# An adaLN block with windowed attention and a spatial gMLP on one core: first loads over 128 partitions, wider PV and modulation streams, shared visits to 64-row tiles, and a newly searched issue order

## The chip, the cores and the metric

The kernel runs on one core of one Trainium2 chip. The metric is the time of one execution on the device in microseconds; below, the median of several executions. The profiled span is about 2 us shorter than the time of the same execution.

Most executions ran with TensorE's granted clock at 1.00 of full speed. Some had a lapse in it, and most of those were some 1 to 3 us longer. All traces that the argument rests on have a mean granted clock of 0.998 or more; the two that don't (e2, e7) are marked. The clock record leaves out the first microseconds: in the kernel before it begins at 7.38 us, and up to there that kernel started its 512-column matmuls 0.427 us apart, later 0.216. "Cold" and "warm" below are names for these two rates. Each batch of experiments ran on one chip, with executions of the kernel before in between; the three batches (e1 to e4, e5 to e8, e9 to e12) ran on three chips. The first batch had no changed kernel beside it, so its runs are compared by their ratio to the kernel before.

## The reference, cut to what matters

```python
# S = 2048 tokens, D = 448, 16 heads of 28, window 256
mod = silu(c) @ w_mod                     # six vectors of 448
sa, ca, ga, sb, cb, gb = mod
h = layernorm(x) * (1 + ca) + sa
x = x + ga * (windowed_causal_attention(h @ wqkv) @ wo)
h = layernorm(x) * (1 + cb) + sb
z = gelu(h @ w_in)                        # 1792 columns
z1, z2 = z[:, :896], layernorm(z[:, 896:])
g = w_sp @ z2 + b_sp                      # 2048 x 2048 over the tokens
return x + gb * ((z1 * g) @ w_out)
```

bfloat16 throughout.

## The kernel before

The program is a graph of some 1,500 named operations. A planner picks an engine and a place for each, by a table of priorities found by search (`PLAN`, 1,473 lines); every engine then runs its list in order. A new table therefore is a new issue order on every engine.

Feature chunks are four of 112 rows. Weights are loaded over 112 partitions:

```python
def wload(name, prio, dst, w, a, b, o=None, ks=(0, KC), eng="sp"):
    src = w[ks[0] * KP:ks[1] * KP, a:b].rearrange("(c p) n -> p c n", p=KP)   # KP = 112, KC = 4
    ...
x_load(0, 2, -90)
t_wmA = mload("wmodA", -89.9, 0, 2)                                   # modulation, columns 0 and 1
t_wqk = [wload("wqk0", ...), wload("wqk1", ...)]
x_load(2, 4, -89.6); t_wv = wload("wv", -89.35, ...); x_load(4, 8, -89.4)   # in the order of these priorities: x tiles 4 to 7 before wv
```

TensorE runs 15 warm-up matmuls in one piece, the first modulation (32 matmuls of one column), then 5 more. The weighted sums of attention (PV) stream 29 columns, 28 of V and one of ones.

After attention comes what I call the **z stage**: the two halves of `h @ w_in`. The features 0 to 383 are three full-height matmuls per output tile. The last 64 rows (the *rest*) of two output tiles run side by side in the two 64-row halves of the array: the two matmuls of a pair start 3 to 4 ns apart, and with 448 columns a pair takes 0.19 to 0.20 us, where one full-height stream takes 0.189. A stay in the 64-row mode is a *visit*:

```python
def unit(name, pr, outs, n):          # outs: four output tiles; z2m = second half, z1m = first half
    for i, (ten, sub, lhs, rhs, ...) in enumerate(outs):      # parts name_0 .. name_3
        for kc in range(3): mm(..., lhs(0, 128, kc), rhs(0, 128, kc), kc == 0, False)
    # then name_r, the rest, ends all four accumulations
    for i, ... in enumerate(outs):
        p0 = 64 * (i % 2)
        mm(..., lhs(p0, p0 + 64, 3), rhs(p0, p0 + 64, 3), False, True, tile_position=(p0, 0))
```

The **mixer** follows: 448 matmuls of 512 columns (`w_sp @ z2`), and the 112 of the output product.

The softmax here doesn't subtract the row's maximum and nothing guards it: scores larger than these inputs give would overflow.

Of the kernel before, what the change touches and what calls it, by code (L numbers as in the profile page):

```python
# [5 lines left out]
BF16 = mybir.dt.bfloat16  # L6
# [238 lines left out]
c -173.9192 -1  # L245
x0 -178.4461 -1
wmodA -9.5493 -1
wqk0 -85.9193 -1
wqk1 -146.8247 -1
x2 -221.2408 -1  # L250
wv -106.8604 -1
x4 -53.1809 -1
wmodG -38.8077 -1
wo -96.1295 -1
x8 -204.0347 -1
x12 -87.9443 -1
wmodB0_0 -132.3998 1
wmodB0_1 -108.5096 25
wmodB0_2 -147.1130 13
wmodB0_3 -114.1850 25  # L260
wmodB1_0 -138.0143 22
wmodB1_1 -43.9367 8
win0_0 -76.8442 26
win0_64 -80.4809 33
win1_0 -191.2469 4
win1_64 -169.0191 13
win2_0 -98.4862 7
win2_64 -58.2163 0
win3_0 -78.8290 14
win3_64 -9.8098 40  # L270
wout0 -55.9687 44
wout1 -0.2256 35
wout2 -220.9180 31
wout3 -169.1615 41
wz -132.5927 -1
id1 85.2723 -1
id2 26.3866 -1
nh -98.3075 -1
xpad -185.4513 -1
wqk0m -43.1282 -1  # L280
va1 -109.7318 -1
opad -127.2002 -1
dsilu -214.1979 -1
silu -77.6433 -1
dexp -98.0973 -1
scr1 -60.2104 -1
warm0 35.9475 -1
modA -36.2363 -1
warm1 -16.3154 -1
modAe0 4.7110 -1  # L290
modAe1 -30.8303 -1
gateA 30.4838 -1
wog0 -52.7600 -1
wog1 129.5466 -1
wog2 20.8828 -1
wog3 -105.6927 2
wqkc0 -106.7042 -1
wqkc1 -99.4673 -1
wqkc2 64.2122 -1
wqkc3 -24.9916 -1  # L300
l1_0st0 -65.9727 -1
l1_0ag -12.7322 -1
l1_0ve -55.7842 -1
l1_0rs -22.6614 -1
xn0 18.1777 -1
l1_1st0 34.6470 -1
l1_1ag -80.7040 -1
l1_1ve 1.4062 -1
l1_1rs -59.9654 -1
xn1 -73.4046 -1  # L310
tr0_0_0 -75.9896 -1
tr0_0_1 -88.3166 -1
hT0_0 41.5631 -1
tr0_1_0 -171.6096 -1
tr0_1_1 43.3804 -1
hT0_1 42.2614 -1
tr0_2_0 -146.6143 -1
tr0_2_1 -8.7731 -1
hT0_2 73.1086 -1
tr0_3_0 36.1564 -1  # L320
tr0_3_1 -15.9541 -1
hT0_3 -16.1573 -1
qk0_0_0 -23.3584 -1
qk0_0_1 -19.3486 -1
qk0_0_2 -26.0578 -1
qk0_0_3 -169.2100 -1
qke0_0 -62.0930 -1
qk0_4_0 -171.1839 -1
qk0_4_1 -124.5527 -1
qk0_4_2 -143.9112 -1  # L330
qk0_4_3 -61.6511 -1
qke0_4 -108.6858 -1
qk0_1_0 -15.9474 -1
qk0_1_1 30.7340 -1
qk0_1_2 -9.1455 -1
qk0_1_3 29.9306 -1
qke0_1 -85.4446 -1
qk0_5_0 74.2985 -1
qk0_5_1 59.0211 -1
qk0_5_2 8.9765 -1  # L340
qk0_5_3 -11.9115 -1
qke0_5 -122.3120 -1
qk0_2_0 11.7421 -1
qk0_2_1 -41.2138 -1
qk0_2_2 -128.5694 -1
qk0_2_3 -161.7595 -1
qke0_2 -104.6116 -1
qk0_6_0 -30.1175 -1
qk0_6_1 -86.6129 -1
qk0_6_2 10.7182 -1  # L350
qk0_6_3 -76.7948 -1
qke0_6 -143.0611 -1
qk0_3_0 46.5935 -1
qk0_3_1 -42.8331 -1
qk0_3_2 -81.0038 -1
qk0_3_3 32.9102 -1
qke0_3 -112.2136 -1
qk0_7_0 -85.2094 -1
qk0_7_1 -4.1600 -1
qk0_7_2 -0.7100 -1  # L360
qk0_7_3 -27.5559 -1
qke0_7 -59.4010 -1
v0_0 -38.6942 -1
v0_1 -126.4105 -1
v0_2 -194.9709 -1
v0_3 -117.1972 -1
ve0 34.4969 -1
v1_0 -63.9484 -1
v1_1 -44.4581 -1
v1_2 -92.9774 -1  # L370
v1_3 6.4639 -1
ve1 -107.1203 -1
l1_2st0 -32.5499 -1
l1_2ag -11.1580 -1
l1_3st0 -1.6855 -1
l1_3ag 19.1541 -1
l1_2ve -42.3370 -1
l1_2rs -58.2673 -1
xn2 0.0606 -1
xn3 -154.1941 -1  # L380
tr1_0_0 163.1188 -1
tr1_0_1 106.8039 -1
hT1_0 -94.2607 -1
tr1_1_0 117.9296 -1
tr1_1_1 -29.4701 -1
hT1_1 -4.3731 -1
tr1_2_0 -133.6710 -1
tr1_2_1 -25.6763 -1
hT1_2 -26.5992 -1
tr1_3_0 19.7744 -1  # L390
tr1_3_1 18.4846 -1
hT1_3 35.9193 -1
qk1_0_0 7.5876 1
qk1_0_1 -17.6342 -1
qk1_0_2 -142.8600 -1
qk1_0_3 -103.8450 -1
qke1_0 -74.8876 -1
qk1_4_0 -17.0046 -1
qk1_4_1 -96.3530 -1
qk1_4_2 65.6313 0  # L400
qk1_4_3 -71.1276 -1
qke1_4 -32.0874 -1
qk1_1_0 -71.2539 -1
qk1_1_1 -156.5775 -1
qk1_1_2 27.2832 -1
qk1_1_3 -25.5604 -1
qke1_1 97.4437 -1
qk1_5_0 61.7763 -1
qk1_5_1 17.2054 -1
qk1_5_2 90.4057 -1  # L410
qk1_5_3 130.8681 1
qke1_5 -86.5170 -1
qk1_2_0 -13.2948 -1
qk1_2_1 12.7524 -1
qk1_2_2 8.2383 -1
qk1_2_3 -146.8308 -1
qke1_2 -29.0645 -1
qk1_6_0 -81.6047 0
qk1_6_1 -77.4223 -1
qk1_6_2 -80.3767 -1  # L420
qk1_6_3 -97.2127 -1
qke1_6 -21.7535 -1
qk1_3_0 -0.6191 -1
qk1_3_1 -25.7692 -1
qk1_3_2 21.7977 -1
qk1_3_3 -69.5120 -1
qke1_3 -126.0368 -1
qk1_7_0 -0.3487 -1
qk1_7_1 8.7945 -1
qk1_7_2 -21.1269 -1  # L430
qk1_7_3 -45.8912 -1
qke1_7 -149.6500 -1
v2_0 1.1530 0
v2_1 -57.3270 -1
v2_2 -142.9541 -1
v2_3 -81.5399 -1
ve2 20.4670 -1
v3_0 22.2004 -1
v3_1 -87.3124 -1
v3_2 -138.9806 -1  # L440
v3_3 17.2187 1
ve3 -79.2309 -1
l1_4st0 -52.7128 -1
l1_4ag -59.1243 -1
l1_5st0 -37.8153 -1
l1_5ag 15.6180 -1
l1_4ve 78.8929 -1
l1_4rs -51.5084 -1
xn4 59.2949 -1
xn5 -41.9947 -1  # L450
tr2_0_0 75.5747 -1
tr2_0_1 33.3240 3
hT2_0 -25.4605 -1
tr2_1_0 -50.8189 -1
tr2_1_1 44.6117 -1
hT2_1 10.8153 -1
tr2_2_0 31.9594 -1
tr2_2_1 72.5624 -1
hT2_2 -13.7090 -1
tr2_3_0 103.6410 3  # L460
tr2_3_1 16.5843 -1
hT2_3 -11.7007 -1
qk2_0_0 -87.7995 -1
qk2_0_1 73.7230 -1
qk2_0_2 111.0347 -1
qk2_0_3 -24.0508 -1
qke2_0 -194.7111 -1
qk2_4_0 47.9921 -1
qk2_4_1 9.5302 1
qk2_4_2 76.1273 3  # L470
qk2_4_3 64.6272 0
qke2_4 -68.4157 -1
qk2_1_0 74.6320 -1
qk2_1_1 9.9189 -1
qk2_1_2 59.6146 -1
qk2_1_3 74.6154 3
qke2_1 -163.3990 -1
qk2_5_0 43.4070 -1
qk2_5_1 35.5826 -1
qk2_5_2 27.3553 1  # L480
qk2_5_3 85.5673 3
qke2_5 -74.8529 2
qk2_2_0 156.0173 5
qk2_2_1 40.1146 5
qk2_2_2 73.0654 -1
qk2_2_3 133.0675 3
qke2_2 -93.0968 -1
qk2_6_0 -115.0317 5
qk2_6_1 -119.5676 -1
qk2_6_2 -160.9855 -1  # L490
qk2_6_3 -51.3236 5
qke2_6 -223.7691 -1
qk2_3_0 112.5395 2
qk2_3_1 46.8260 -1
qk2_3_2 -49.0943 -1
qk2_3_3 -64.1020 0
qke2_3 -130.1151 2
qk2_7_0 -146.7712 5
qk2_7_1 3.6711 2
qk2_7_2 -13.5238 -1  # L500
qk2_7_3 -95.2462 -1
qke2_7 -199.6110 0
v4_0 152.7729 -1
v4_1 135.2634 -1
v4_2 157.2010 -1
v4_3 145.1857 -1
ve4 -214.0459 -1
v5_0 2.4442 5
v5_1 -34.8380 -1
v5_2 132.6977 5  # L510
v5_3 49.2850 -1
ve5 199.1028 -1
l1_6st0 6.1606 -1
l1_6ag -84.8142 -1
l1_7st0 16.3026 -1
l1_7ag 21.6624 -1
l1_6ve 25.2248 -1
l1_6rs -109.8818 -1
xn6 129.1957 -1
xn7 -94.4319 1  # L520
xnT6 -102.6968 -1
xnT7 78.1329 -1
hT3_0 9.5317 1
hT3_1 -57.6889 -1
hT3_2 -16.7000 -1
hT3_3 37.2559 -1
qk3_0_0 42.0666 11
qk3_0_1 46.8950 3
qk3_0_2 62.4591 -1
qk3_0_3 100.2217 10  # L530
qke3_0 140.8824 4
qk3_4_0 12.1190 -1
qk3_4_1 24.7900 -1
qk3_4_2 15.1879 7
qk3_4_3 6.0524 -1
qke3_4 155.7109 -1
qk3_1_0 -12.9199 14
qk3_1_1 63.1581 -1
qk3_1_2 78.8401 6
qk3_1_3 117.3578 -1  # L540
qke3_1 86.3928 2
qk3_5_0 158.9730 3
qk3_5_1 111.0073 4
qk3_5_2 132.4676 -1
qk3_5_3 23.7719 -1
qke3_5 53.2656 8
qk3_2_0 -14.5477 9
qk3_2_1 -38.2804 8
qk3_2_2 89.0201 -1
qk3_2_3 98.7245 -1  # L550
qke3_2 68.9811 -1
qk3_6_0 40.1905 -1
qk3_6_1 -103.6586 -1
qk3_6_2 -82.9275 2
qk3_6_3 -169.4196 1
qke3_6 67.1570 3
qk3_3_0 97.5666 7
qk3_3_1 136.9780 -1
qk3_3_2 42.4361 -1
qk3_3_3 94.1988 -1  # L560
qke3_3 114.7131 -1
qk3_7_0 -136.2301 -1
qk3_7_1 -126.8240 -1
qk3_7_2 -79.6186 -1
qk3_7_3 -155.7894 0
qke3_7 101.1398 -1
v6_0 45.1656 -1
v6_1 30.8966 -1
v6_2 1.8837 -1
v6_3 0.9966 -1  # L570
ve6 -14.1774 -1
v7_0 107.9714 -1
v7_1 34.0811 -1
v7_2 -81.3353 8
v7_3 45.4250 -1
ve7 101.7989 -1
l1_8st0 -25.8323 -1
l1_8ag 47.3158 2
l1_9st0 -34.4816 2
l1_9ag 120.4231 -1  # L580
l1_10st0 81.0417 -1
l1_10ag 18.6453 -1
l1_11st0 99.4861 -1
l1_11ag 41.7120 -1
l1_8ve 34.1898 -1
l1_8rs 14.9445 5
xn8 -98.6791 -1
xn9 75.3490 -1
xn10 -107.0961 -1
xn11 -88.2281 3  # L590
xnT8 35.9566 5
xnT9 -141.0896 6
xnT10 11.1342 -1
xnT11 46.1012 -1
hT4_0 -91.4517 12
hT4_1 -91.5522 6
hT4_2 -29.0111 7
hT4_3 -100.8445 -1
qk4_0_0 67.2637 12
qk4_0_1 94.0035 16  # L600
qk4_0_2 168.4363 -1
qk4_0_3 121.9014 -1
qke4_0 -60.2725 -1
qk4_4_0 -97.3372 -1
qk4_4_1 -102.6324 -1
qk4_4_2 -65.4026 5
qk4_4_3 -97.4252 10
qke4_4 -79.9073 5
qk4_1_0 -0.8298 17
qk4_1_1 88.3774 -1  # L610
qk4_1_2 109.3984 5
qk4_1_3 65.1619 7
qke4_1 -56.7742 18
qk4_5_0 18.6271 -1
qk4_5_1 -57.0070 4
qk4_5_2 -47.9674 -1
qk4_5_3 1.7263 11
qke4_5 -75.7541 8
qk4_2_0 73.7239 15
qk4_2_1 -52.7726 12  # L620
qk4_2_2 79.4371 -1
# [1854 lines left out]
```

## Time and profile before

| | kernel before |
|---|---|
| median, runs | 283.48 us (283.03 to 283.94, 4 runs) |
| first projection, first exponential start | 11.32, 16.02 us |
| last block of 16 score matmuls starts, last exponential ends | 111.47, 113.86 us |
| first mixer matmul starts, last result computed | 158.52, 278.52 us |
| ScalarE idle just before exponentials (with 0.6 us for the first scores) | 5.3 us |

The prediction shows the chain, the windows and the head. One more view: where ScalarE waited during attention. In its timeline of the kernel before (start, length, instruction, count, and in brackets the idle time just before and what ended it), these are the pieces after 60 us that began with a wait:

```profile
66.84 8.48 ACT L2172 ACTIVATE PT<-ps 128x1024 bf16<-128x1024 f32 x9 [0.36 <-PE ps L1940]
75.63 10.19 ACT L2172 ACTIVATE PT<-ps 128x1024 bf16<-128x1024 f32 x11 [0.31 <-PE ps L1940]
86.13 16.84 ACT L2172 ACTIVATE PT<-ps 128x1024 bf16<-128x1024 f32 x18 [0.31 <-PE ps L1940]
103.46 7.44 ACT L2172 ACTIVATE PT<-ps 128x1024 bf16<-128x1024 f32 x8 [0.49 <-PE ps L1940]
111.92 1.94 ACT L2172 ACTIVATE PT<-ps 128x1024 bf16<-128x1024 f32 x2 [1.03 <-PE ps L1940]
```

Each bracket is a place where TensorE had other work between two score blocks and ScalarE ran dry. They sum to 2.5 us. Before 60 us there are six more, 2.8 us, not counting the wait for the first scores; three of these stand before evacuations and not before exponentials.

### The profile page before, as it was taken

To read this page: it belongs to the slowest core of one execution; us is meant where nothing else is said; L and a number is where in the kernel's file an instruction comes from. 1 tells how busy PE (TensorE), PEld (TensorE's weight loads), DVE (VectorE), ACT (ScalarE), POOL (GpSimd) and SP (SyncE) were. 2 spreads that over 40 slices of the span, in tenths; PEclk is the share of its full clock that TensorE was granted. 3 is DMA by queue.
4 is the path that set the end of the run, shared out by engine and by line. 5 is a ranking of instruction groups with operands and counts; after the bars stand their busy time and mean duration, and the time that the engine had idled before them with its cause. 6 is when DMAs were issued, how large, how long until landed. Compare 5 with 4: busy or idle time off the path is not lost.

```text
span 280.8 us, 6444 instructions
## 1 busy us (share of the span) xinstructions
PE 268.1 (95%) x2669; PEld 136.8 (49%) x2684; DVE 173.1 (62%) x439; ACT 128.1 (46%) x171; POOL 64.7 (23%) x110
## 2 busy tenths in 40 slices
PE   7879998999999989999989999999999999999995
PEld 2656755645555745534334344444444444454452
DVE  4599869768787898999888712232314044425335
ACT  4388899999999998936654500002000000000000
POOL 5041425454544748113131300000000000000000
PEclk9999999999999999999999999999999999999999
DMA  6994272963484466668999994000000000011113
GB/s 168 270 267 80 57 134 40 161 69 23 86 144 98 105 92 124 96 136 134 183 204 183 187 194 75 2 0 0 2 0 0 0 2 0 0 33 52 34 33 114
DMA packets 66300, 25.15 MB, mean 90 GB/s; under 512 B 57504, under 2 KB 65632, under 8 KB 66272
## 3 DMA queue, kind: packets, MB, share of 16 engines
q1 hardware_dynamic: 66144, 24.75, 46.3%
q8 instruction: 21, 0.34, 0.6%
q14 instruction: 7, 0.06, 0.1%
q10 hardware_dynamic: 128, 0.00, 0.0%
HBM read 9.01 MB, written 1.84 MB: 39 GB/s over the span
## 4 chain that ended last, share of the span: by engine, by line
PE 80%; ACT 7%; DMA 6%; DVE 3%; issue 2%; SPq 0%; DVEq 0%
PE ps L1940 80%; ACT PT L2172 6%; DMA oT<-o_sb 3%; DMA wqk_raw<-in_A_wqkv_dram 3%; DVE hT L2076 1%; ACT QKT L2110 1%; DVE Vaug L2133 1%; DVE o_sb L2205 0%; ACT hT L2060 0%; SPq L1878 0%; DVE WQK L2086 0%; DVE QKT L2113 0%; DVE fin L2405 0%; DVE hT L2064 0%; DVE rec_all L2202 0%
## 5 line engine op out<-in xcount | busy, mean ns | idle before, releaser
L2172 ACT ACTIVATE PT<-ps 128x1024 bf16<-128x1024 f32 x90 | 84.8, 1046 | 5.3 <-PE ps L1940 4.9
L1940 PE MATMUL ps<-w_spA,z 128*128 128x512 bf16 x329 | 76.4, 379 | 0.4
L2383 DVE TENSOR_TENSOR tmpg<-ps,bsp_bc 128x512 bf16<-128x512 f32 x28 | 19.3, 691 | 65.9 <-PE ps L1940 65.9
L1940 PEld LDWEIGHTS ps<-w_spA,z 128*128 128x128 bf16 x336 | 32.8, 98 | 39.6 <-PE ps L1940 0.4
L2181 POOL TENSOR_SCALAR_AFFINE_SELECT PT<-PT 128x512 f32<-128x512 f32 x60 | 38.3, 646 | 41.3 <-ACT PT L2172 41.1
L2010 POOL TENSOR_TENSOR rs_all<-ve_all,neghalf 128x1 f32<-128x1 f32 (+2 forms) x39 | 24.3, 631 | 54.3 <-DVE ve_all L2008 52.0
L1940 PE MATMUL ps<-hT,WQK 112*128 112x256 bf16 (+1 forms) x192 | 33.9, 308 | 2.5 <-ACT hT L2060 0.9
L2362 ACT ACTIVATE z1T<-ps 128x512 bf16<-128x512 f32 x28 | 14.4, 611 | 39.5 <-PE ps L1940 39.5
L1940 PE MATMUL ps<-w_spB,z 128*128 128x512 bf16 x109 | 27.8, 379 | 0.1
L1940 PE MATMUL ps<-hT,w_in_sb 128*128 128x512 bf16 (+1 forms) x108 | 23.0, 380 | 1.3 <-PE ps L1940 1.0
L1940 PE MATMUL ps<-w_in_sb,hT 128*128 128x448 bf16 (+1 forms) x128 | 24.2, 353 | 0.0
L1940 PE MATMUL ps<-w_out_sb,z1T 128*128 128x448 bf16 x112 | 22.0, 352 | 0.0
L1940 PEld LDWEIGHTS ps<-hT,WQK 112*128 112x128 bf16 x192 | 16.6, 97 | 11.2 <-PE ps L1940 2.8
L1940 PE MATMUL ps<-Vaug,PT 128*128 128x29 bf16 x720 | 21.8, 175 | 0.1
L1940 PEld LDWEIGHTS ps<-Vaug,PT 128*128 128x128 bf16 x720 | 20.3, 97 | 3.1 <-PE ps L1940 0.4
L2014 DVE BATCH_NORM_STATS2 st_all<-x_sb 128x6 f32<-128x448 bf16 x32 | 19.4, 616 | 2.5 <-DMA x_sb<-in_A_x_dram 2.4
L1940 PE MATMUL ps<-QKT 32*128 32x128 bf16 x720 | 18.2, 216 | 1.9 <-ACT PT L2172 1.2
L2113 DVE CAST QKT<-ps 128x512 bf16<-128x512 f32 (+1 forms) x27 | 15.3, 569 | 6.4 <-PE ps L1940 6.3
L1940 PEld LDWEIGHTS ps<-QKT 32*128 32x128 bf16 x720 | 10.7, 92 | 16.1 <-PE ps L1940 13.6
L1940 PEld LDWEIGHTS ps<-w_spB,z 128*128 128x128 bf16 x112 | 10.9, 98 | 13.2
L1940 PE MATMUL ps<-wo_sb,oT 112*128 112x448 bf16 x64 | 15.7, 352 | 1.3 <-DMA oT<-o_sb 1.0
L1940 PEld LDWEIGHTS ps<-w_in_sb,hT 128*128 128x128 bf16 (+1 forms) x128 | 9.8, 97 | 13.1 <-issue 3.5
(58 smaller groups left out, 240.0 us busy)
## 6 DMA issues: line engine op xcount, KB each, us to landing
w_in_sb<-in_B_w_in_dram SPq DMA_DIRECT2D x8, 224.0 KB, 4.5
out_dram<-fin SPq DMA_DIRECT2D x16, 112.0 KB, 1.7
x_sb<-in_A_x_dram SPq DMA_DIRECT2D x3, 448.0 KB, 10.1
wmod_sb<-in_w_mod_dram SPq DMA_DIRECT2D x6, 196.0 KB, 3.8
wmod_sb<-in_w_mod_dram SPq DMA_DIRECT2D x1, 784.0 KB, 7.0
wqk_raw<-in_A_wqkv_dram SPq DMA_DIRECT2D x2, 392.0 KB, 8.3
w_out_sb<-in_B_w_out_dram SPq DMA_DIRECT2D x3, 224.0 KB, 3.1
bsp_bc<-in_B_b_sp_dram SPq DMA_DIRECT2D x1, 512.0 KB, 5.4
```

The lines of the kernel that those rows point to most:

```text
L1940: return e.matmul(out_, lhsT=lhsT, rhs=rhs, start=st, stop=sp, **kw)
L2010: return P.op(name + "rs", prio, [("pool", 515 + 150 * (t1 - t0 - 1), lambda e: e.tensor_tensor(rs_all[:, slot, t0:t1], ve_all[:, slot, t0 ...
L2014: st = [P.op("%sst%d" % (name, i), prio, [("dve", dve_ns(D, base=65), lambda e, i=i, s_=s_: e.bn_stats(st_all[:, slot, t, i, :], s_()))], ...
L2076: return e.tensor_scalar(hT[0:KP, cc, t0 * 128:t1 * 128], hT[0:KP, cc, t0 * 128:t1 * 128], modT[0:KP, 4 + cc:5 + cc], modT[0:KP, cc:cc + 1 ...
L2110: return e.activation(QKT[:, g, t0 * 128:t1 * 128], ps[:, ten.slot, 0:n], ACT.Copy)
L2113: return e.tensor_copy(QKT[:, g, t0 * 128:t1 * 128], ps[:, ten.slot, 0:n])
L2133: return e.tensor_copy(Vaug[:, t, :, 0:DH], ps[:, ten.slot, 0:D].rearrange("p (h d) -> p h d", d=DH))
L2172: return e.activation(PTb[:, pt.slot].rearrange("p g q i -> p (g q) i"), ps[:, ten.slot:ten.slot + 2, :].rearrange("p i n -> p n i"), ACT. ...
L2181: return e.affine_select(out=v, in_=v, pattern=[[0, 4], [s_, 128]], compare_op=ALU.is_ge if diag else ALU.is_gt, fill=0.0, base=0, channel ...
L2362: z1_op[(ft, tb)] = P.op("z1g%d_%d" % (tb, ft), pr, [("act", act_ns(512), lambda e, tb=tb, ft=ft, ten=ten: e.activation(z1T[:, ft, tb * 51 ...
L2383: a = P.op("ga%d_%d" % (tb, ft), pr, [("dve", 610, lambda e, tb=tb, ten=ten, tg=tg: e.tensor_tensor(tmpg[:, tg.slot, :], ps[:, ten.slot, : ...
```

## The change

The intent: get the first weights over all 128 partitions, fix the order of the loads only up to the weights of V, break the warm-up into pieces, keep TensorE's streams wide, enter the 64-row mode less often, and search a new order for all of it. The core of the diff (cuts marked; in the table, all 1,458 names that both share got new values):

```diff
-WARM = (15, 5)
+REST_AHEAD = tuple("z1m%d" % u for u in range(0, 28, 4))
+PVN = 50
+MODN = 96
+WARM = (11,)                     # pieces of two matmuls each
...
-    def wload(...): ... w[ks[0] * KP:ks[1] * KP, a:b].rearrange("(c p) n -> p c n", p=KP)
+    def rows4(name, prio, dst, w, a, b, o=None):          # three chunks of 128 rows, then 64 rows
+        ...
+        return [load(name + "a", prio, ... dst[:, 0:3, ...]), load(name + "b", prio + 0.001, ... dst[0:64, 3, ...])]
...
-    x_load(2, 4, -89.6)          # then x tiles 4 to 7, wv, x tiles 8 to 11, wmodG, wo, in this fixed order
+    t_wmA = rows4("wmodA", ...); t_wqk = rows4("wqk", ...); x_load(2, 4, -89.7); t_wv = rows4("wv", ...)
+    for a_, b_ in zip(loads[:n_first], loads[1:n_first + 1]):
+        b_.order.append(a_)      # fixed order up to wv; what follows is free
...
-        w = KP if ... else 128;  ... sc_sb[0:KP, kc:kc + 1]           # modulation, 1 column
+        w = 64 if ... else 128;  ... sc_rep[:, kc, 0:MODN]            # 96 columns
...
-                            last = mm(e, ps[:, pv_ten.slot, 32 * h:32 * h + DH + 1], PTb[...], Vaug[:, kb, h, 0:DH + 1], ...)
+                            n = DH + 1 if h % 4 == 3 else PVN
+                            last = mm(e, ps[:, pv_ten.slot, 32 * h:32 * h + n], PTb[...], <n columns from Vaug[:, kb, h, 0]>, ...)
...
     def unit(name, pr, outs, n):
+        ahead = name in REST_AHEAD
+        if ahead:                # the rest opens the four accumulations instead of ending them
+            parts.append(P.op("%s_r" % name, ..., alloc=[o[0] for o in outs if o[5]], table="row"))
...
-        return P.op("%s_r" % name, ...)          # all four tiles are done with the rest
+        if ahead:
+            return parts[1:]                      # each tile is done with its own last part
```

The loads behind V's weights are now placed by the search. In the planned order the visits go from 15 to 11: the rest of z2 units 12, 8, 14 and 10 is followed at once by the rest of z1 units 0, 16, 12 and 24.

## The prediction

> **What bounds the kernel now.** I read the chain of waits first, then the timeline by engine, then windows. The chain that ended last is four fifths TensorE, and from 118.67 us to the end it hardly leaves it:
>
> ```profile
> PE 80%; ACT 7%; DMA 6%; DVE 3%; issue 2%; SPq 0%; DVEq 0%
> ```
>
> The windows (window, length, then busy us of PE, PEld, DVE, ACT, POOL, granted clock, DMA share, GB/s) cut the run where its limits change: head, first projections and scores, early attention, three stretches of attention, the z stage (z1, z2), the mixer (G) with the output product.
>
> ```profile
> 0.00:11.30 11.30, 8.83 (x59) 4.04 (x60) 4.58 (x16) 3.76 (x7) 4.10 (x13) 1.00 0.79 202
> 11.30:16.00 4.70, 4.10 (x49) 3.36 (x50) 4.67 (x15) 2.91 (x9) 0.70 (x1) 1.00 1.12 284
> 16.00:30.00 14.00, 12.65 (x179) 8.93 (x179) 13.60 (x43) 12.70 (x22) 5.36 (x8) 1.00 0.63 135
> 30.00:60.00 30.00, 28.56 (x523) 17.05 (x521) 22.63 (x54) 28.24 (x34) 12.45 (x20) 1.00 0.66 103
> 60.00:90.00 30.00, 29.53 (x574) 16.31 (x574) 24.54 (x58) 28.69 (x32) 14.98 (x24) 1.00 0.49 82
> ...
> 118.60:151.90 33.30, 31.98 (x168) 13.02 (x170) 29.65 (x93) 17.47 (x30) 8.46 (x14) 1.00 0.91 160
> 151.90:281.00 129.10, 125.42 (x591) 57.58 (x600) 48.17 (x94) 7.38 (x12) 2.52 (x5) 1.00 0.21 44
> ```
>
> So there are three limits. Head: nothing is saturated, loads are waited for. Attention, 16 to 113.9 us: ScalarE (90 exponentials, 0.94 us from start to start), with VectorE full up to 30 us and TensorE near full. After the last scores (111.47 us): TensorE. The last stretch is work that the change leaves alone: G is 448 streams of 512, the output product 112 of 448. From chain pieces like "10.74 us x49" a 512 stream costs 0.216 to 0.219 us; at 0.216 and 0.189 they need 96.8 + 21.2 = 118.0 us. What can move is when the last score matmul runs, and what TensorE loses between it and the start of G.
>
> The head, from the chain in order of time (start, us, what): the query-key weights land at 9.83, and only then does VectorE reach the modulation columns, which wait behind two weight copies in its queue.
>
> ```profile
> 2.07 7.76 DMA wqk_raw<-in_A_wqkv_dram
> 9.83 0.02 issue
> 9.85 0.70 DVE WQK L2086 x2
> 10.55 0.07 DVE modT L1986
> 10.62 0.08 DVE modT L1985
> 10.70 0.03 issue
> 10.72 0.55 DVE hT L2064
> ```
>
> The z stage, from TensorE's timeline (start, us, instruction, wait):
>
> ```profile
> 137.86 2.93 PE L1940 MATMUL ps<-w_in_sb,hT 128*128 128x448 bf16 x16
> 141.75 3.07 PE L1940 MATMUL ps<-hT,w_in_sb 128*128 128x512 bf16 x15 [0.96 <-PE ps L1940]
> ```
>
> and VectorE's in the same place:
>
> ```profile
> 139.54 1.68 DVE L2014 BATCH_NORM_STATS2 st_all<-z2rB 128x6 f32<-128x448 bf16 x3
> 141.13 0.30 DVE L2259 TENSOR_SCALAR hT<-hT,modT 128x128 bf16<-128x128 bf16 x1
> ```
>
> The 0.96 us hole is put down to TensorE, but its next weight load starts at 141.50, just after VectorE's last piece of hT ended at 141.43. I read it as a wait for that piece, which stood behind three statistics instructions. ScalarE waited there too, but only because tiles come in fours: a z1 group is finished by its shared K=64 rest.
>
> [...] windows of 1 us give 243 to 297 GB/s from 4 to 11 us, when 112-partition weights land, and 361 from 11 to 12, when a 128-partition x load is due.[...] 48 PV matmuls (29 columns) start at 97.04 and the next work at 98.25, 25.2 ns each[...].[...] The 15 warm-up matmuls took 6.30 us, 0.42 each, so they were all cold[...]; the ones after the modulation ran warm.[...] In the trace, two z2 units from 111.81 to 116.49 hold 18 full streams and 4 row-tiled pairs, 22 x 0.189 = 4.16 us, and took 4.68: 0.26 per visit. Another unit (148.84 to 151.92) holds 14 streams, 2.65, and took 3.08: 0.43.
>
> **The change part by part.**
>
> *Loads.* Modulation and query-key weights are 803 KB each; before, they come over 112 partitions at about 266 GB/s, 6.0 us for both. After, 688 KB of each comes over 128 partitions, which I put at 340 GB/s, between 266 and 361, and 115 KB over 64 rows at 266: 2 x (2.02 + 0.43) = 4.9 us. So the second lands some 1.1 us sooner, the first 0.55. That isn't gained in full: TensorE's queue has 14 warm-up matmuls (6.0 us at 0.427) before the modulation, and still 8 (1.7 us warm) plus four transposes between it and the first projection. Start of warm-up 1.4 + 6.0 + c by matmul 0.2 + transposes 0.3 = modulation at 7.9 (8.31 before). 32 matmuls of 96 columns at 42 ns are 1.35 us (1.06 before), so it ends at 9.25 against 9.37. With 8 warm-ups and transposes, projections start at 11.2 (11.32 before). Also all four hT evictions of block 0 are now on ScalarE, 0.46 each in series, two engines before; against that two of eight QKT evictions go to VectorE, 2 x 0.33 off ScalarE. First exponential: 0.4 us sooner, give or take 0.6.
>
> *Padding to 128 rows.* Contraction over 128 instead of 112 rows costs no stream time: the 128- and 112-row groups of 448 columns both read 352 to 353 ns. The zero fills run on VectorE before x lands (idle 2.39 us there). c as one row costs four tiny matmuls and a second SiLU, beside the wait for weights.
>
> *PV from 29 to 50 columns.* 540 of 720 matmuls grow[...]: 0 us.[...]
>
> *The new order in attention.* The numbers of exponentials and projections are the same; the schedule puts 20 instead of 21 QKT evictions on ScalarE, 3 Vaug as before, 7 hT instead of 6. ScalarE was idle about 6 us between 12.95 and 113.9, 3.4 of it from 15 to 37 us. A better order can win some of it, never more. I take 0.5 us, between -1 and +2.
>
> *z rests.* All z1 groups now do the K=64 rest first, and in four places it follows a z2 rest directly: 11 visits instead of 15. 4 x 0.26 to 0.43 = 1.0 to 1.7, say 1.2 us. z1 tiles then finish one by one, which spreads the GELUs. In the new VectorE order the last pieces of hT come ahead of the next tile's statistics, so about half of the 0.96 us hole goes, 0.5.
>
> Sum: 0.4 + 0.5 + 1.2 + 0.5 = 2.6; 283.9 - 2.6 = 281.3.
>
> **Rivals.** *A: the head counts in full.* If the clock turns warm early and the weights land 1 to 2 us sooner, everything moves by that: about 280. For it: everything after is a chain, so it isn't swallowed. Against: the warm-ups and transposes ahead of the projections. *B: hidden anyway.* If ScalarE's and VectorE's early queues set the attention, and a wait for z2's normalisation or the transposed spatial weights replaces the visits, time stays at 283 to 284. For it: VectorE was 97% busy from 16 to 30; DMA share 0.91 in the z stage; the new order starts G with a chunk that needs second-half spatial weights at once, where the old one asks for them some 7 us into G. Against: those transposes are issued a few places earlier now. *C: cold clock.* If the 96-column modulation runs cold it costs 32 x 80 ns = 2.6 us, and the following 8 warm-ups 3.4 instead of 1.7: 285 to 286. For it: 6.3 us cold before. Against: warm by 9.5 us before[...].
>
> **Range and chances.** The last 118 us are fixed, so the gain is bounded by head (2), idle ScalarE (some 3 realistically) and z stage (2.5); all together would be 276.5, which is unlikely. Over 2% needs a gain of 5.7. I take 278.5 to 283.5; 10% faster by over 2%, 88% within, 2% slower.
>
> **What would show it.** Right: first exponential at 15.2 to 16.0 (16.02); modulation matmuls about 42 ns apart; PV still near 25 ns; last score matmul 0.5 to 1.5 us sooner than 111.47; from there to the first G matmul (158.52) about 1.7 us less; the distance from first G to the end unchanged within 0.3. Wrong: first exponential before 14.8 (A); a DMA wait before the first G, or ScalarE idle as before with the z stage no shorter (B); warm-up or modulation streams at half rate past 9 us (C).

Passages are cut from it where marked: statements of how the hardware behaves that no trace or run of this case shows. No term of the sum is among them. That 50 columns would cost no more than 29 was my assumption. The trace before shows matmuls of 1 and of 29 columns starting 25 ns apart, and nothing for 50. The 340 GB/s is my estimate, put between the 266 (the mean of the seven windows from 4 to 11 us) and the 361 of that trace; that 64 rows come at 266 is one too. The 42 and 80 ns of a 96-column matmul are estimates too; 0.216 and 0.427 us per 512 columns would make 40.5 and 80. Some readings differ from the trace: the 0.94 us of an exponential is 16.84 us over 18, while they start 0.92 us apart at the median; a query-key eviction on ScalarE takes 0.31 us (eight in 2.48), not 0.33; and "nothing is saturated" holds for the mean of the head (DMA share 0.79), but from 5 to 11 us that share reads 1.03 to 1.12.

## The result, and the profile after

The changed kernel took **280.63 us** (median of 4 runs, 280.18 to 280.79) against 283.48. All outputs are right. The ratio is 0.9897, with a 95% interval of 0.9872 to 0.9922. A ratio here is the mean time of one kernel's fast runs over that of the other's in the same rounds, so it isn't quite the ratio of the medians. The same kernel ran twice more beside the experiments: 280.36 us, ratio 0.9918 (0.9889 to 0.9947), and 280.07 us, 0.9894 (0.9867 to 0.9922).

So the gain is 1%, within the predicted range and on the predicted side. But it did not come from where I expected it. From the traces (us):

| | before | after | after, 2nd trace | after, 3rd trace |
|---|---|---|---|---|
| first exponential starts | 16.02 | 16.32 | 16.15 | 16.55 |
| first exponential to end of last | 97.84 | 94.87 | 94.82 | 95.22 |
| last score block to last result | 167.05 | 167.70 | 166.93 | 167.14 |
| of it, to the first mixer matmul | 47.05 | 49.00 | 48.23 | 48.44 |

(The last row isn't like for like: the kernel before left one z1 part and a rest for after its first mixer matmul.) The head gained nothing, the z stage gained nothing, and attention gained 3 us.

The chain of waits of the changed kernel, as shares of its span, answers to the chain line in the prediction. ScalarE is gone from it, and a load of x has taken the place of the query-key weights:

```profile
PE 88%; DVE 5%; DMA 3%; SPq 2%; issue 1%; DVEq 0%
```

The windows of the changed kernel, cut at its own events (columns as in the prediction: window, length, busy PE, PEld, DVE, ACT, POOL, clock, DMA share, GB/s):

```profile
0.00:11.65 11.65, 9.38 (x67) 4.52 (x68) 7.31 (x23) 4.37 (x9) 4.17 (x15) 1.00 0.88 250
11.65:16.30 4.65, 4.08 (x49) 3.33 (x50) 3.71 (x12) 2.94 (x8) 0.70 (x1) 1.00 1.10 336
...
30.00:60.00 30.00, 29.24 (x541) 17.66 (x540) 26.15 (x65) 29.33 (x36) 12.29 (x19) 1.00 0.36 77
60.00:90.00 30.00, 29.84 (x612) 17.01 (x611) 24.37 (x60) 29.73 (x34) 17.18 (x30) 1.00 0.62 115
...
111.20:157.80 46.60, 45.09 (x285) 19.49 (x282) 38.49 (x118) 29.86 (x45) 9.16 (x16) 1.00 0.90 162
157.80:278.80 121.00, 118.03 (x561) 54.68 (x559) 43.19 (x81) 0.79 (x2) 1.13 (x2) 1.00 0.11 28
```

Read the ACT column (ScalarE): from 30 to 60 us it is busy for 29.33 us, 28.24 before; from 60 to 90 for 29.73, 28.69 before. The bytes do move faster in the head (250 against 202 GB/s), yet the first projection comes at 11.65 us, 0.33 later than before.

ScalarE's timeline of the changed kernel, the pieces after 35 us that began with a wait, against the five above:

```profile
37.35 1.94 ACT L2226 ACTIVATE PT<-ps 128x1024 bf16<-128x1024 f32 x2 [0.26 <-PE ps L1993]
109.25 1.94 ACT L2226 ACTIVATE PT<-ps 128x1024 bf16<-128x1024 f32 x2 [0.79 <-PE ps L1993]
```

Between these two, from 37 to 109 us, the timeline lists no wait of ScalarE. Counting exponentials in the two traces tells where the gain lies: after the first, the 31st starts 38.35 us later before and 37.06 after, the 90th and last 96.83 and 93.85. So 1.3 of the 3.0 us are won up to the 31st, where the waits went from 2.8 to 1.8 us, and 1.7 behind it, where they went from 2.5 to 0.8.

The head of the changed kernel, VectorE's timeline:

```profile
9.55 0.70 DVE L2140 COPY WQK<-wqkv_raw 128x896 bf16<-128x896 bf16 x2 [2.43 <-DMA wqkv_raw<-in_A_wqkv_dram]
10.17 0.21 DVE L2042 TENSOR_SCALAR modT<-ps 128x3 f32<-128x3 f32 x2
10.30 0.15 DVE L2040 COPY modT<-ps 128x4 f32<-128x4 f32 x1
10.37 0.38 DVE L2140 COPY WQK<-wqkv_raw 64x896 bf16<-64x896 bf16 x1
10.79 1.16 DVE L2070 BATCH_NORM_STATS2 st_all<-x_sb 128x6 f32<-128x448 bf16 x2
...
11.95 0.36 DVE L2140 COPY WQK<-wqkv_raw 128x896 bf16<-128x896 bf16 x1
```

The modulation matmuls ended at 8.92 us, but their result stands at 10.17 behind two weight copies that start at 9.55, when the weights have landed. The last weight copy stands behind two statistics. And the chain in order of time shows that this doesn't even set the end:

```profile
7.21 7.43 DMA x_sb<-in_A_x_dram
14.63 0.02 issue
14.65 1.16 DVE st_all L2070 x2
```

The path goes through the load of x tiles 4 to 7 and VectorE's work on them. In the kernel before VectorE started these statistics at 13.71, without a wait: there this load was issued at 4.10 us and landed at 13.56, here, behind V's weights and others, at 7.21 and 14.63.

The z stage of the changed kernel, TensorE's timeline, all pieces between the last scores and the mixer that began with a wait:

```profile
109.72 4.64 PE L1993 MATMUL ps<-w_in_sb,hT 128*128 128x448 bf16 x26 [0.53 <-DVE mv_all L2073]
...
120.41 0.73 PE L1993 MATMUL ps<-w_in_sb,hT 128*128 128x448 bf16 x3 [0.50 <-PE ps L1993]
...
132.76 1.30 PE L1993 MATMUL ps<-w_in_sb,hT 128*128 128x448 bf16 x6 [1.01 <-PE ps L1993]
```

Two us of holes, where the timeline of the kernel before lists one of 0.96 and two of 0.16. But these are too long. Counted against the issue order, 4 of the 283 matmul records of that stage are missing in the trace before, and none in the three traces of the changed kernel. Three of the four stood just behind these holes. The last is an example, a z1 part of three matmuls: three weight loads, from 151.69, but two matmuls.

```profile
151.69 0.33 PEld L1940 LDWEIGHTS ps<-hT,w_in_sb 128*128 128x128 bf16 x3 [0.37 <-issue]
151.92 0.59 PE L1940 MATMUL ps<-hT,w_in_sb 128*128 128x512 bf16 x2 [0.16 <-issue]
```

Less the 0.22 us of a missing matmul each, one hole of some 0.74 us is left. What stands behind the last hole of the changed kernel is in VectorE's timeline and in the DMA queue's (three spatial-weight transposes, then the transpose of token tile 9):

```profile
131.27 1.38 DVE L2315 TENSOR_SCALAR hT<-hT,modT 128x512 bf16<-128x512 bf16 x4 [2.16 <-DMA hT<-xn]
```
```profile
123.07 4.49 SPq L2339 DMA_TRANSPOSE w_spA<-in_B_w_sp_dram  x3
127.60 1.26 SPq L2287 DMA_TRANSPOSE hT<-xn  x1
```

VectorE had normalized that tile by 121.49 us, but its transpose was issued at 127.60, behind the weights.

### The profile page after: what moved, and what is told of

The parts are those of the page before. It is cut to its first block, busy times and chain, and to the rows that moved or that the text cites. A ratio compares the mean times of both kernels' runs of the same rounds, so it can differ in the third digit from the quotient of the medians.

```text
span 278.8 us, 6473 instructions
## 1 busy us (share of the span) xinstructions
PE 268.7 (96%) x2690; PEld 137.4 (49%) x2690; DVE 174.7 (63%) x445; ACT 129.4 (46%) x172; POOL 63.5 (23%) x112
## 4 chain that ended last, share of the span: by engine, by line
PE 88%; DVE 5%; DMA 3%; SPq 2%; issue 1%; DVEq 0%
PE ps L1993 88%; DMA x_sb<-in_A_x_dram 3%; DVE st_all L2070 1%; SPq L1904 1%; SPq L1903 1%; DVE hT L2130 1%; DVE x_sb L2277 1%; DVE hT L2118 0%; DVE o_sb L2261 0%; SPq L1911 0%; DVE QKT L2167 0%; DVE ve_all L2064 0%; DVE fin L2470 0%; DVE gb_sb L2321 0%; DVE mv_all L2073 0%
## 5 line engine op out<-in xcount | busy, mean ns | idle before, releaser
L2066 POOL TENSOR_TENSOR rs_all<-ve_all,neghalf 128x1 f32<-128x1 f32 (+2 forms) x39 | 23.4, 610 | 53.6 <-DVE ve_all L2064 53.3
L1993 PE MATMUL ps<-hT,WQK 128*128 128x256 bf16 (+1 forms) x192 | 33.7, 308 | 1.2 <-ACT hT L2114 0.7
L1993 PE MATMUL ps<-w_spB,z 128*128 128x512 bf16 x112 | 28.4, 379 | 0.0
L1993 PE MATMUL ps<-hT,w_in_sb 128*128 128x512 bf16 (+1 forms) x112 | 23.8, 380 | 0.0
L1993 PE MATMUL ps<-Vaug,PT 128*128 128x50 bf16 (+1 forms) x720 | 21.9, 181 | 0.0
L1993 PEld LDWEIGHTS ps<-hT,WQK 128*128 128x128 bf16 x192 | 16.5, 97 | 9.5 <-PE ps L1993 1.9
L2427 ACT ACTIVATE z1T<-ps 128x512 bf16<-128x512 f32 x28 | 16.0, 602 | 6.5 <-PE ps L1993 6.0
L1993 PE MATMUL ps<-wo_sb,oT 128*128 128x448 bf16 x64 | 15.8, 353 | 0.9 <-PE ps L1993 0.6
```

The costliest lines, as they stand in the source:

```text
L1993: return e.matmul(out_, lhsT=lhsT, rhs=rhs, start=st, stop=sp, **kw)
L2066: return P.op(name + "rs", prio, [("pool", 515 + 150 * (t1 - t0 - 1), lambda e: e.tensor_tensor(rs_all[:, slot, t0:t1], ve_all[:, slot, t0 ...
L2427: z1_op[(ft, tb)] = P.op("z1g%d_%d" % (tb, ft), pr, [("act", act_ns(512), lambda e, tb=tb, ft=ft, ten=ten: e.activation(z1T[:, ft, tb * 51 ...
```

## The experiments

My theory after these traces: (1) the new order of attention alone makes the gain; (2) the head is bound elsewhere, by VectorE's queue and then by the load of x tiles 4 to 7; (3) four visits fewer do save TensorE time, and new holes take it back. Rivals: the wider PV or the earlier loads made the gain; visits cost nothing because other engines bind the z stage.

For all experiments the planner's result was written out as a list (operation, engine, buffers) and replayed, so that single operations could be moved and nothing else would move with them. In the replay of an unedited kernel each engine runs the same instructions in the same order as in the kernel itself. The edits are moves in these lists. An order in this sense includes the engine and the buffers of each operation; these were not parted.

### e1: the new attention order on the kernel before

```diff
 kernel before: its head, its loads, its 29-column PV, its z stage
-order of the operations from the first query-key projections to the last scores: its own
+the same operations in the order and buffers of the changed kernel
```

> The kernel before (its loads over 112 partitions, its warm-up, PV of 29 columns, modulation of 1 column, its z stage with 15 visits and rests behind) with one thing taken from the changed kernel: the instruction order of the attention on all engines, from the first query-key projections to the last score matmul, written out as a fixed list. Theory (the gain of 2.85 us is the new order, which keeps ScalarE fed): last exponential 2 to 3 us sooner than 113.86 us, ScalarE's idle time before exponentials 2 to 3 us instead of 5.3, time 280.5 to 281.8, about the changed kernel's 280.63. Rival (loads, wider PV or z rests carry the gain, the order only fits them): 283 to 284.5, as the kernel before or slower, since the order was made for other landing times.

Measured: 281.08 us (279.89 to 282.8, 6 runs) against 282.71, ratio 0.9945 (0.9914 to 0.9977). In the trace, first exponential to end of last took 95.45 us (97.84 before, 94.82 to 95.22 in the changed kernel), and ScalarE's waits, without that for the first scores, sum to 3.1 us (5.3 and 2.6). Last score matmul to end: 166.78, as before. ScalarE's pieces after 35 us that began with a wait are now these:

```profile
37.61 1.94 ACT L2198 ACTIVATE PT<-ps 128x1024 bf16<-128x1024 f32 x2 [0.19 <-PE ps L1966]
55.70 5.84 ACT L2198 ACTIVATE PT<-ps 128x1024 bf16<-128x1024 f32 x6 [0.23 <-PE ps L1966]
109.70 1.94 ACT L2198 ACTIVATE PT<-ps 128x1024 bf16<-128x1024 f32 x2 [0.79 <-PE ps L1966]
```

So the order alone, without any other part of the change, gives 2.4 of the 3.0 us of attention in these traces, and some 0.55% of time. That is half of the 1.0% of the whole change, but the interval reaches from 0.2 to 0.9%; whether the other parts add to it on balance is not shown.

### e2: PV back to 29 columns

```diff
-PVN = 50
+PVN = 29
```

> The changed kernel with the same fixed order, PV streams back at 29 columns instead of 50. Theory[...]: PV starts stay 25 ns apart, 280.63 within 0.3 us. Rival[...]: a change of over 0.7 us either way, with matmul spacings that differ in the attention.

Measured: 280.34 us (279.18 to 283.06, 6 runs), ratio 0.9933 (0.9896 to 0.997); the changed kernel's own ratios elsewhere were 0.9894 to 0.9918, so the intervals overlap and no difference is shown; one of under 1 us could hide in them. The traces are sharper: PV matmuls start 25 ns apart in both, and from the 31st to the 69th exponential, where neither trace has a wait, e2 took 36.32 us and the changed kernel 36.33. The profiled run was the slowest of the six, with a mean clock of 0.993. Its windows of TensorE (window, length, busy, clock, DMA share, GB/s) show why:

```profile
91.00:92.00 1.00, 1.00 (x46) 1.00 0.68 158
...
93.00:94.00 1.00, 1.00 (x3) 0.50 0.06 6
94.00:95.00 1.00, 1.00 (x19) 0.50 0.57 88
95.00:96.00 1.00, 1.00 (x4) 0.50 0.37 143
```

The granted clock fell to half for some 3.4 us in the middle of dense work, and ScalarE waited 0.34 and 0.85 us for scores just after (0.97 us near 36 us have another cause: VectorE had waited 1.07 us for a load of x just before, in e5 0.28). This isn't a property of the edit. A mean clock of 0.987 to 0.994, which I take for the same lapse, once or twice, came in 5 of the 33 executions of the kernel before that ran beside the experiments, and in 1 of 6 each of e1 and e2, all with 29-column PV; in none of 16 of the changed kernel, but with 50 columns also in one of six each of e3, e6 and e8, and in two of e7. Whether the wider PV makes it rarer stays open.

### e3: z1 rests behind again, units in one piece

```diff
-REST_AHEAD = tuple("z1m%d" % u for u in range(0, 28, 4))
+REST_AHEAD = ()
 TensorE order: each z1 unit at the place where it began, parts 0 to 3 and then its rest, 15 visits
```

> The changed kernel with the same fixed order, but every z1 group has its K=64 rest behind its four full parts, in one piece, so there are 15 visits to row tiling and no shared ones (11 in the changed kernel). My prediction's figure of 0.26 to 0.43 us a visit: 1.0 to 1.7 us slower than 280.63, so 281.7 to 282.4. Rival (visits stand beside waits for VectorE and the transposes of hT, which set the z stage; the trace after shows holes of 0.50, 0.53 and 1.01 us there): within 0.5 us of 280.63, holes changing in size against the visits.

Measured: 286.95 us (286.17 to 288.9), ratio 1.0164 (1.0133 to 1.0195). Attention was unchanged (last score matmul at 108.58), but from there to the end took 173.76 us, 6 to 7 more than the changed kernel. TensorE's waits in that stretch before the mixer sum to some 6.4 us (without three of 0.16 that are missing records again), against 2.0; 2.7 of them are waits for ScalarE's GELU of z1, because all four tiles of a unit finish, and give back their banks, together. So this run says little of visits: it shows that with this order the early rests are needed so that tiles finish one by one. It doesn't repeat the kernel before, which mixed parts of different units.

### e4: the modulation ahead of the weight copies

```diff
 VectorE order
-wqkc1 wqkc0 modAe1a modAe1b modAe0 wqkc3 l1_2st0 l1_3st0 l1_2ag wqkc2
+modAe1a modAe1b modAe0 wqkc1 wqkc0 wqkc3 l1_2st0 l1_3st0 l1_2ag wqkc2
 warm-up: three pieces (6 matmuls) fewer after the modulation
```

> The changed kernel with the same fixed order, except that VectorE evacuates the three modulation pieces before the two weight copies that wait for the query-key weights, and that 6 of the 8 warm-up matmuls behind the modulation are gone. Theory (the head counts in full: everything after it is a chain): first projection at 10.4 instead of 11.65 us, first exponential 0.8 to 1.2 us sooner than 16.32, time 279.5 to 279.9. Rival (early VectorE work and the landing of x set the attention's start, so a sooner first exponential is given back by 30 us): 280.3 to 280.9. A third:[...] projections at 213 ns instead of 109, and the time rises by 1 us or more.

Measured: 280.7 us (278.91 to 281.71), ratio 0.9927 (0.9893 to 0.996). The first projection came at 10.45 us (11.05 to 11.88 in six traces with the head of the changed kernel), but the first exponential at 16.04, no sooner than the mean of those six (16.1, see e5): TensorE stopped after seven projections and waited 0.74 us for the weight copy that stood behind statistics. So the rival had the time right. The third didn't happen: projections start 109 ns apart.

### e5 and e9: the changed kernel again

> The changed kernel itself, with its instruction order fixed as it was (each engine runs the same instructions in the same order), as the measure for the runs beside it: about 280.6 us where the kernel before takes 283.5, a ratio of 0.990. If the unclear runs of the first batch came from a restless chip and not from the kernels, this one shows the size of that unrest.

> The changed kernel with its order fixed, again as the measure on this chip: ratio to the kernel before 0.990 to 0.992, last score matmul to first spatial matmul 48.2 to 49.0 us with the same three holes of TensorE (0.59 us after the last score matmul, 0.2 to 0.7 near 120, 0.8 to 1.2 near 132).

Measured: 280.36 us (279.75 to 280.98) and 280.07 us (279.44 to 280.8). Their traces are the 2nd and 3rd of the table. They also tell how much one trace is worth: with the identical head (the changed kernel's three, e2, e3, e6) the first exponential came at 16.32, 16.15, 16.55, 15.72, 16.14 and 15.75 us, mean 16.1; with the head of the kernel before at 16.02 and, in e1, 16.19. The 0.3 us that the head seemed to lose is scatter. What is shown is that it gained nothing.

### e6: the four shared visits parted

```diff
 TensorE order, four times alike
-z2m12_1 z2m12_2 z2m12_3 z2m12_r z1m0_r z1m0_0 z1m0_1
+z2m12_1 z2m12_2 z2m12_3 z1m0_r z1m0_0 z2m12_r z1m0_1
```

> The changed kernel with its four shared visits of the 64-row matmuls parted again: the rest of z2 tile 12, 8, 14 and 10 goes one z1 group of three matmuls later, so that full-height matmuls stand between it and the z1 rest; z1 rests still ahead of their units. 15 visits in place of 11, nothing else moved. My theory (each visit costs 0.26 to 0.43 us and TensorE bounds the z stage): last score matmul to first spatial matmul 1.0 to 1.7 us longer than 49.0, the whole 281.7 to 282.3. Rival (the z stage waits for the elementwise engines, so the visits are hidden): within 0.3 us of the changed kernel, with the holes before TensorE shorter by as much.

Measured: 282.43 us (281.57 to 285.49, 6 runs), ratio 1.0006 (0.9963 to 1.0048), 2.1 us over the changed kernel on the same chip. Last score matmul to first mixer matmul: 50.43 us against 48.23. One of the four places in TensorE's timeline:

```profile
154.30 1.36 PE L2019 MATMUL ps<-hT,w_in_sb 64*128 64x512 bf16 x7
155.60 0.55 PE L2019 MATMUL ps<-w_in_sb,hT 64*128 64x448 bf16 x4
156.08 2.12 PE L2019 MATMUL ps<-hT,w_in_sb 128*128 128x512 bf16 x9
158.70 7.07 PE L2019 MATMUL ps<-w_spA,z 128*128 128x512 bf16 x32 [0.51 <-PE ps L2019]
```

The z1 rest with the next z1 part (4 + 3 matmuls), then the z2 rest by itself, then the other z1 parts: two visits where there was one.

The start times of single matmuls give the price of a visit cleanly. Full-height streams of 448 columns start 0.189 us apart; the last one before a rest takes 0.285. Inside a visit a pair of 448-column rests takes 0.186 to 0.199; the last pair before a full-height stream takes 0.281. For 512 columns it is 0.216 and 0.312 on the way in, and 0.308 on the way out. So a visit costs 0.096 going in and about 0.09 coming out, **0.19 us**, and four cost 0.76. Most of the rest of the 2.2 us is waits: in this stretch TensorE's waits sum to 2.3 us, 1.2 in the run beside it. One is the last line of the fence; I read it so that the rest that ends the z2 tiles comes later, and their banks with it. Both theories were half right: the visits aren't hidden, and they cost half of what I had put.

### e7: the old attention order on the changed kernel

```diff
 changed kernel: its head, its loads, its 50-column PV, its z stage
-order of the operations from the first query-key projections to the last scores: its own
+the same operations in the order and buffers of the kernel before
```

> The changed kernel (its head, its loads, its 50-wide PV, its z stage) with the attention stage in the order of the kernel before. Theory (the order is what shortened attention): last exponential ends near 113.9 plus 0.3 instead of 111.2, ScalarE's waits for PT near 5 us instead of 2.4, the whole 2 to 3 us longer than the changed kernel, about 283.2. Rival (the 50-wide PV or the earlier loads shortened it, and the order only follows): last exponential near 111.5, the whole within 0.7 us of the changed kernel.

Measured: 286.8 us (284.74 to 289.83, 6 runs), ratio 1.0136 (1.0087 to 1.0185). The profile: mean clock 0.993, the lapse near 140 us; up to 120 us its clock was 1.00, and there ScalarE waited 6.3 us for scores (4.9 in the kernel before). So without the new order the rest of the change doesn't gain but loses, more than expected. I take it that an order is found for given landing times and durations, and that the old one no longer fits; that is not tested. How the extra 3 us divide I can't say from this profile: besides the lapse its first loads came late (the first piece of the query-key weights at 10.71 us, at 8.93 to 9.77 in the other traces with these loads), so its first exponential started at 17.75. From there to the end of the last one, all at full clock, it took 99.96 us, 2.1 more than the kernel before.

### e8: the head put right

```diff
 VectorE order
-wqkc1 wqkc0 modAe1a modAe1b modAe0 wqkc3 l1_2st0 l1_3st0 l1_2ag wqkc2
+modAe1a modAe1b modAe0 wqkc1 wqkc0 wqkc3 wqkc2 l1_2st0 l1_3st0 l1_2ag
 warm-up: as e4
```

> The changed kernel with the head put right on VectorE: the three copies of the first modulation go ahead of all four WQK copies, and the last two WQK copies go ahead of the statistics of x tiles 2 and 3; six warm-up matmuls fewer after the modulation, as in the earlier run. Theory (the first projection waited for WQK copies that stood behind statistics): no hole inside the first 32 projection matmuls, first exponential at 15.2 to 15.4 us instead of 16.3, and the whole about 1.0 us under the changed kernel if the later stages keep their length. Rival (attention is fed by later loads, so a sooner start is given back as waits for them): first exponential as said, the last one still near 111, the whole within 0.3 us.

Measured: 280.01 us (278.95 to 284.01, that one left out of the ratio), ratio 0.9892 (0.986 to 0.9925), against 280.36 for the changed kernel beside it. The first exponential came at 15.11 us, a full us sooner; the last one ended at 110.87, against 110.97. The gain was given back. VectorE's timeline:

```profile
14.36 1.15 DVE L2093 BATCH_NORM_STATS2 st_all<-x_sb 128x6 f32<-128x448 bf16 x2 [0.52 <-DMA x_sb<-in_A_x_dram]
```

VectorE stood idle for the load of x tiles 4 to 7, and from there ran the same queue at the same times as in e5 (statistics at 14.36 and 14.31, first evacuation of transposed tiles at 17.13 and 17.11).

### e10 to e12: the holes, both stages, and the load

```diff
 e10, changed kernel: DMA queue
-h2T12 h2T11 h2T13 wsp0_0 wsp1_0 oT15 h2T8 wsp2_0 wsp3_0 wsp4_0 h2T9
+h2T12 h2T13 h2T11 wsp0_0 wsp1_0 oT15 h2T8 h2T9 wsp2_0 wsp3_0 wsp4_0
 and VectorE order
-x1_13 rec14 l2_13st0 nrm14
+rec14 nrm14 x1_13 l2_13st0
-h2M12_2 l3_4st0 h2M12_1
+h2M12_2 h2M12_1 l3_4st0
 e11 = e10 and e8
 e12 = e11, and in the DMA queue
-wva wvb woa wmodGb x4
+wva wvb x4 woa wmodGb
```

> The changed kernel with four moves of issue order in the z stage and nothing else: the transposing DMA of token tile 9 ahead of the three spatial-weight loads it stood behind; that of tile 13 ahead of tile 11; on VectorE the last modulation of tiles 12 and 13 ahead of a statistics pair, and the normalization of the 15th attention output ahead of the residual of the 14th tile. Theory (the four visits saved 0.19 us each by the trace's start-to-start times, and three new holes gave it back): the holes near 109, 120 and 132 go, last score matmul to first spatial matmul 46.8 to 47.4 us, the whole 1.0 to 1.7 us under the changed kernel. Rival (TensorE's holes are only where a later limit shows, such as ScalarE's gelu that frees the banks): the holes move to other places, the stage within 0.4 us of 48.2.

> The head of e8 and the four moves of e10 together. Theory (two stages one after the other, but the sooner head is given back at the landing of x tiles 4 to 7): first exponential 15.1, last exponential near 110.9 all the same, the whole as e10 within 0.4 us. If instead the two gains add, 2.0 to 2.7 us under the changed kernel.

> e11 with the load of x tiles 4 to 7 issued before the output-projection weights and the second half of a modulation load (about 1.2 us sooner in the queue). Theory (after the head was put right, VectorE stood at 14.36 us for this load, and its statistics, normalizations and evacuations then ran without a gap at the same times as in the changed kernel): these statistics start near 13.2 to 13.5 us, the last exponential ends 0.6 to 1.0 us sooner, near 110.1, the whole 0.5 to 1.0 us under e11. Rival (VectorE's work per tile or TensorE bounds those microseconds, not the load): last exponential unchanged within 0.2 us.

Measured, beside e9 with 280.07 us: e10 279.78 (278.9 to 280.27, ratio 0.9878), e11 279.95 (279.41 to 280.19, 0.9887), e12 279.71 (277.87 to 281.08, 0.9889). By the traces the moves did what they were meant to, if not always by as much. In e10 the holes near 120 and 132 us are gone and the first one has moved to the next unit, so last scores to mixer took 47.59 us, 0.6 to 1.4 less than in the three traces of the changed kernel and a little more than the 46.8 to 47.4 expected:

```profile
111.33 2.92 PE L2019 MATMUL ps<-w_in_sb,hT 128*128 128x448 bf16 x16 [0.61 <-PE ps L2019]
```

In e12 VectorE no longer waits for the load; its statistics start at 13.40 (13.95 in e11, with a wait of 0.38), and the last exponential ends at 109.70 instead of 110.57, as the theory said (the load landed at 12.54 us, in e11 at 13.93):

```profile
13.40 1.14 DVE L2093 BATCH_NORM_STATS2 st_all<-x_sb 128x6 f32<-128x448 bf16 x2
```

But in e11 new holes of 0.38 and 0.21 us stood near 139 us, and its stage took 48.77. Over six runs each, the medians of all four kernels lie within 0.4 us and all intervals overlap. So I can't claim that any of them beats the changed kernel; the profiled run of e12, 277.87 us, is the fastest seen, and others of it took 281.

## Why the prediction was right or wrong, by its own steps

**The number** (281.3, measured 280.63) was right by luck: of the four terms of the sum three brought nothing, and the fourth, put at 0.5 us, brought it all. In the two first traces: head +0.30, attention -2.97, from the last score matmul on +0.65, together -2.02 us, where the ends lie 2.03 us apart (278.52 and 276.49). Of the prediction's signs of being right two held, 42 ns between modulation matmuls and 25 ns in PV. The others did not: the first exponential came at 16.32 us, the last scores 2.7 us sooner and not 0.5 to 1.5, from there to the first mixer matmul it took 1.95 us more and not 1.7 less, and from that matmul to the end 1.3 less, where no change was expected (the z1 part behind it before).

**Head, 0.4 us: measured 0.0, with a scatter of some 0.4.** The loads did what was predicted, and more. The rate rose (299 against 255 GB/s from 2 to 12 us); the first modulation weights were complete at 6.50 us (8.26 before) and the query-key weights at 10.27 (11.47 before; predicted was "some 1.1 us sooner"). Why the rate rose stays open: the partitions, the pieces and the order of the loads changed together. The modulation matmuls did as predicted, 42 to 43 ns apart, and ended at 8.92, sooner than predicted. The step that failed first is "projections start at 11.2". It follows TensorE's queue, and I had not followed VectorE's, although the prediction itself shows the modulation behind two weight copies there. What these two wait for is only the first piece of the query-key weights, two chunks of four before and three now, and this piece came 0.3 us sooner (9.53 against 9.83). So the first projection came at 11.65, in six traces at 11.05 to 11.88. e4 and e8 show that this queue held it. The second failed step is rival A's "everything after is a chain, so it isn't swallowed": e8 made the first exponential a full us sooner and the last one 0.1 us; the chain ran through the x load, which the change itself had put back, and e12 shows it by moving it forward.

**PV, 0 us: right.** Matmuls of 50 columns start 25 ns apart, as those of 29 and of one column did (those of 96: 42 to 43), and e2 shows no difference.

**Attention order, 0.5 us: measured 3.0, of which the order alone makes 2.4 (e1).** I had named the right place, idle ScalarE, and a range of -1 to +2; the size failed. I treated its waits as something that a search would only nibble at. But each of them ended with a result of TensorE, most with a score block, and the order sets when these come. The new one has no wait from 37 to 109 us and 1.0 us less before.

**Visits, 1.2 us: 0.76 by the price measured, and nothing in the stage.** The step that failed is the price, "0.26 per visit" and 0.43. Start times of single matmuls give 0.19. I had divided the time from group to group, and that holds other things: in the first case 0.10 us behind the second visit that other visits don't show, in the second the stream of the missing matmul (0.22 us) that the fence on the z stage shows. TensorE did bound the stage enough for the price to count (e6), but the new order brought 1.2 to 2.0 us of waits where the old had some 0.7. The account closes: the kernel before took 47.05 us and 1.30 for the z1 part behind its first mixer matmul, 48.35; less 0.76 for the visits, plus 0.4 to 1.3 for the waits makes 48.0 to 48.9, and the three traces show 48.23 to 49.00.

**The 0.96 us hole (some 0.74 without the missing record), half of it, 0.5 us: it went, and others came.** The reading, a wait for VectorE's last piece of hT, fits what followed: the new hole of 1.01 us ends with such a piece too, only that VectorE itself waited for a transpose queued behind spatial weights. Moving that transpose and its like (e10) removed it. Rival B, a wait that replaces the visits, is thus what happened in the z stage alone; a DMA wait before the first mixer matmul, which I had given as its sign, did not appear. Rival C, cold modulation, did not happen.

## What to carry to other kernels

When an engine that sets a stage shows many small waits in the middle of it, add them up: the sum is what a better order can win there, and here it was worth more than every local saving. Before counting an earlier load as a gain, follow the queue of each engine that handles its data, and ask which load the same engine waits for next. Price a mode switch or any short cost from start times of single instructions, not from lengths of groups; count the records against the program, since some can be missing (here 4 of 283 in one stage); and then look for the wait that will take its place.

## What the traces show of the hardware

- Entering the 64-row mode cost 0.096 us and leaving it about 0.09, at the median of the visits in each trace, with 448- or 512-column streams.
- The 512-column matmuls of the mixer, each with a weight load, start 216 ns apart in both kernels, through some 97 us of them.
- The first full-rate warm-up started 3.45 to 5.93 us after the first matmul in the traces of the changed kernel's head (3.45 in e2, 5.93 in e7, with the same warm-up), and 5.92 and 5.95 us after it in the two traces with the head of the kernel before.
- In e2 the granted clock was 0.50 for about 3.4 us while TensorE was busy without a gap in the profile (1.00 us of each us from 91 to 96). In e7 its mean was 0.89 from 135 to 150 us, which would be 3.3 us at half, and a hole of 2.21 us ends in that stretch, at 139.99. What brings the lapse is open.
